# Block-sparse attention with a gated projection: the first weight chunks a unit later, fewer queries at first, and the loads of later batches spread over other units

## The chip, the cores and the metric

The kernel runs on one core of a Trainium2 chip. A time is device microseconds (us) of one launch. The core's engines are named as in the profile: PE (matrix multiplications, with PEld for its weight loads), DVE (the vector engine), ACT (the scalar engine), POOL (the general engine) and SP, which does no arithmetic and issues DMA transfers.

## The reference, cut to what matters

```python
# q, k, v: (B=4, H=8, S=768, D=64); 24 blocks of 32 rows
mask = np.abs(blk_i - blk_j) <= 1
mask = mask | (blk_i == 0) | (blk_j == 0) | (blk_i == n_blocks - 1) | (blk_j == n_blocks - 1)
for qb in range(n_blocks):
    for kb in sampled_blocks[qb]:                     # 3 of them
        mask[qb * block:(qb + 1) * block, kb * block:(kb + 1) * block] = True
scores = np.where(mask, scale * (q @ k^T), -1e9)
attn = softmax(scores)
x = (attn @ v).transpose(0, 2, 1, 3).reshape(B, S, 512)

gate_pre = sum(conv_w[k] * xp[:, k:k + S, :] for k in range(5))   # xp: x, padded by 4 rows ahead
gate = 1 / (1 + np.exp(-gate_pre))
out = (gate * (x @ w_val)) @ w_out                    # w_val, w_out: 512 x 512
```

A query block sees the two end blocks (0 and 23), its own neighbourhood and three sampled blocks. The two end blocks see everything. The result goes through a causal convolution over five rows that makes a gate, and two projections.

## The kernel before

**Units.** The work goes in 52 units. One unit is a pair of neighbouring query blocks with all eight heads; the two end blocks of a batch make two units of their own, which read all the keys and values of the batch. Batch 0 has units 0 to 12, with the end blocks first (0, 1). Batch 1 has 13 to 25, batch 2 has 26 to 38, batch 3 has 39 to 51; in these the end blocks come after four pairs (units 17 and 18, 30 and 31, 43 and 44). The step loop (L684 to L752) runs over units. In step n it issues loads, the scores of unit n, the copies of keys for unit n + 2 (COPY_AHEAD), the values of unit n - 2, and the transposes of unit n - 1; between these come the jobs of the gate and the projections (`fill`, `prepare`); then it scales the queries of unit n + 2.

**Order.** A small class (InOrder) chains every instruction to the one before it on its engine, so each engine runs its instructions in the order in which the program issues them. All instructions go through it, which is why they all have one line, L77, in the profile. A transfer issued by SP is given one of eight completion semaphores in turn, and its issue waits for the transfer that had that semaphore before, the eighth one back.

**Names.** `k` is the keys of a whole batch, in six chunks; `kg` the group of key blocks of one pair, copied from `k` by several engines. `vn` is the values of a whole batch, which the end blocks need, also in six chunks. `va` holds the value rows of a pair's own neighbourhood, in a ring of four; its first use of each buffer also loads the two end blocks' rows (a transfer of 64x1x520 ahead of one of 64x520). `vb` holds the gathered rows of the sampled blocks, fetched by POOL with an indirect DMA. `qc` is the queries of a pair (five buffers), `sc` and `s` scores, `mx` row maxima, `pe` exponentials, `pt` and `ptr` their transposes, `av` and `x` the attention output.

**Weights.** `w_val`, `w_out` and `conv_w` arrive as float64. Each of the eight 128-row chunks (`wst`, 128x1024 words, 512 KB) is turned on the DVE into a high and a low part (`wv`, `wo`) by the generator at L154, eight instructions on 128x512 per chunk, and one copy on ACT. Two chunks are worked on in turn, one step of each; the convolution's weights (`cst`) are first. A chunk's steps can begin DECODE_LAG units after its load was issued (L204 to L224), and the first step of all waits for a unit as well. `prepare(steps)` takes two steps at each of its two calls in a unit, three in units 2 to 6, so four or six in a unit. A chunk of `w_out` reuses the buffer of a chunk of `w_val` and is loaded when that one is decoded. When all are decoded, the same calls go on to the gate and the projection.

**Loads.** What is loaded when is set by tables of unit numbers: KEYS_AT (L32) for a batch's key chunks, ENDS_AT (L33) for its `vn` chunks, WEIGHTS_AT (L40) for the weight chunks. In unit 0 the first pair's keys are loaded and with them the queries of the first QUERIES_FIRST pairs (L41, used at L300); the loop `while more_keys()` at L703 then loads on as far as buffers go. From unit 1 on each step loads the keys, queries and values of the coming pairs as buffers come free.

Of the kernel before, what the change touches and what calls it, by code (L numbers as in the profile page):

```python
# [28 lines left out]
VRING, GRING = 4, 3  # L29

SIXTHS = 6
KEYS_AT = {1: (2, 2, 5, 5, 6, 6), 2: (15, 16, 17, 18, 19, 20), 3: (27, 28, 29, 30, 31, 32)}  # L32
ENDS_AT = {1: (9, 9, 10, 10, 13, 14), 2: (21, 22, 23, 24, 25, 26), 3: (34, 35, 36, 37, 38, 39)}  # L33

GLOB_AFTER = [-1] + [3] * (B - 1)
LAG_T, LAG_V = 1, 2
VALUES_AHEAD = 2

BUSY = (7, 1, 1)
WEIGHTS_AT = (0, 1, 3, 4, 7, 8, 11, 12)  # L40
QUERIES_FIRST = 5  # L41
DECODE_LAG = 3
SCALE_AHEAD = 2
COPY_AHEAD = 2

# [13 lines left out]
def attention_moe(ctx, tc, qb, kb, v, sampled, w_val, conv_w, w_out, ident_in, slot_in, out):  # L59
# [80 lines left out]
    def indices(b):  # L140

        row = const.tile([128, NB], F32, tag=f"row{b % 2}", name="row")
        dve.tensor_scalar_add(row, base, float(b * S - B * S))
        dve.tensor_tensor(out=row, in0=row, in1=valid, op=ALU.mult)
        dve.tensor_scalar_add(idx[:, b, :], row, float(B * S))
# [8 lines left out]
    def decode(hi, lo, raw, n):  # L154

        hw, lw = raw[:, :, 1], raw[:, :, 0]
        t = two.tile([128, DM], F32, tag="ot", name="words").bitcast(I32)[:, 0:n]
        dve.tensor_scalar(out=t, in0=hw, scalar1=0x1FF, scalar2=15, op0=ALU.bitwise_and, op1=ALU.logical_shift_left)
        yield True
        dve.scalar_tensor_tensor(  # L160
            out=lw.bitcast(U32), in0=lw.bitcast(U32), scalar=17, in1=t.bitcast(U32),
            op0=ALU.logical_shift_right, op1=ALU.bitwise_or,
        )
        yield True

        dve.tensor_scalar(out=t, in0=hw, scalar1=0x7FFFFFFF, scalar2=None, op0=ALU.bitwise_and)
        yield True
        dve.tensor_scalar(
            out=t.bitcast(F32), in0=t.bitcast(F32), scalar1=2.0**-15, scalar2=2.0**16, op0=ALU.max, op1=ALU.mult
        )  # L170
        yield True
        dve.tensor_scalar(out=t, in0=t, scalar1=3, scalar2=0x7FFFF000, op0=ALU.logical_shift_left, op1=ALU.bitwise_and)
        yield True
        dve.scalar_tensor_tensor(out=t, in0=hw, scalar=-(1 << 31), in1=t, op0=ALU.bitwise_and, op1=ALU.bitwise_or)
        yield True
        dve.tensor_scalar(out=hw, in0=t, scalar1=-(1 << 23), scalar2=None, op0=ALU.bitwise_and)
        yield True
        dve.scalar_tensor_tensor(out=lo, in0=lw, scalar=2.0**-35, in1=hw.bitcast(F32), op0=ALU.mult, op1=ALU.mult)
        act.copy(hi, t.bitcast(F32))
        yield True  # L180
# [15 lines left out]
    def decode_conv():  # L196
        yield from decode(cwp[:, 0, :], cwp[:, 1, :], cst, CH * KW)
        dve.tensor_tensor(
            out=cw.rearrange("p c k -> p (c k)"), in0=cwp[:, 0, :].bitcast(F32), in1=cwp[:, 1, :].bitcast(F32),
            op=ALU.add,  # L200
        )
        yield True

    def decode_weights():  # L204

        jobs, begun = [(-1, decode_conv())], 0
        while step[0] < DECODE_LAG - 1:
            yield False
        while jobs or begun < 2 * CH:
            n = begun  # L210
            if len(jobs) < 2 and n < 2 * CH and len(staged) > n and step[0] >= staged[n][0] + DECODE_LAG:
                dst = wv if n < CH else wo
                jobs.append((n, decode(dst[0][:, n % CH, :], dst[1][:, n % CH, :], staged[n][1], DM)))
                begun += 1
            if not jobs:
                yield False
                continue
            n, job = jobs.pop(0)
            if next(job, None):
                jobs.append((n, job))  # L220
                yield True
            else:
                decoded.add(n)
        decoded.add("all")  # L224
# [49 lines left out]
    def block_numbers(pr, eng):  # L274

        by = COPIED_FIRST if pr.seq < FIRST_PAIRS else COPIED[pr.bt.b]
        mine = [n for n in range(2 * NR) if by.get(n, SP) == eng]
        if not mine:
            return
        first = NR * PAIRS[pr.p][0] + mine[0]  # L280
        _, regs = nc.values_load_multi_w_load_instructions(
            sm[0:1, first : first + len(mine)], engines=[eng], min_val=0, max_val=NB - 1,
            skip_runtime_bounds_check_because="block numbers are drawn from [0, 24)",
        )
        for n, reg in zip(mine, regs):
            yield 5 + 4 * (n // NR) + n % NR, reg

    def load_queries(pr):
        pr.qc = five.tile([128, HP, 2, BLK], F32, tag="qc", name="qc")
        sp.dma_start(pr.qc, qb[:, pr.bt.b, pr.p + 1])  # L290

    def load_keys(pr):
# [3 lines left out]
        if pr is pairs[0]:  # L296
            for _ in range(3):
                next(keys_of[0])
            sp.dma_start(ident, ident_in)
            for other in pairs[1:QUERIES_FIRST]:  # L300
                load_queries(other)
# [314 lines left out]
    step, numbers_first = [0], {}  # L616
# [46 lines left out]
    def freed(k):  # L663

        return units[min(k, N - 1)].pr.seq if k >= 0 else -1

    def more(which, upto, load):
        if at[which] < len(pairs) and pairs[at[which]].seq <= upto:
            load(pairs[at[which]])
            at[which] += 1  # L670
            return True

    def until(which, n, do):
        while at[which] < min(len(pairs), pairs.index(units[min(n, N - 1)].pr) + 1):
            do(pairs[at[which]])
            at[which] += 1
# [7 lines left out]
    for n in range(N + LAG_V):  # L684
        step[0] = n

        def more_keys():
            return more("keys", freed(n - 1) + RING, load_keys)

        def more_values():  # L690
            free, soon = freed(n - LAG_V - 1), units[min(n + VALUES_AHEAD, N - 1)].pr.seq
            return (
                more("rows", min(free + VRING, soon), load_rows), more("gathered", min(free + GRING, soon), gather)
            )

        if n == 0:
            more_keys()
            indices(0)
            until("scaled", 1, scale)
            for _ in range(3):  # L700
                next(values_of[0])
            sp.dma_start(cst.rearrange("p n w -> p (n w)"), conv_w.bitcast(I32))
            while more_keys():  # L703
                pass
            more("rows", units[VALUES_AHEAD].pr.seq, load_rows)
            numbers_first.update({eng: list(block_numbers(pairs[1], eng)) for eng in (DVE, POOL, ACT)})
        else:
            while more_keys() or any(more_values()):
                more_values()
        store()  # L710
        for b in range(1, B):
            for at_units, loads in ((KEYS_AT[b], keys_of[b]), (ENDS_AT[b], values_of[b])):
                for _ in range(at_units.count(n)):
                    next(loads)
        k = len(staged)
        if k < 2 * CH and n >= WEIGHTS_AT[k] and (k < 4 or k - 4 in decoded):
            next(weights)

        if n == 0:
            none = ps_av.tile([128, 512], F32, tag="av", name="none")  # L720
            keep_busy(none, BUSY[0])
        if n < N:
            later = scores(units[n])
        until("copied", n + COPY_AHEAD, copy_keys)
        if n == 0:
            while any(more_values()):
                pass
        if 0 <= n - LAG_V < N:
            values(units[n - LAG_V])
        steps = STEPS + (n in MORE)  # L730
        if 0 <= n - LAG_T < N:
            for half, _ in enumerate(transposes(units[n - LAG_T])):
                if not (half and n in HELD):
                    fill()
                prepare(steps if half < 2 else 0)
            if later is not None:
                later()
        else:
            fill()
            prepare(steps)  # L740
        if 0 <= n - LAG_V < N and units[n - LAG_V].last:
            pr = units[n - LAG_V].pr
            finish(pr)
            pr.bt.done.add(pr.p)
            for t, (r0, rn) in enumerate(TILES[pr.bt.b]):
                need = {p for p in range(NP - 1) if any(r0 <= i * BLK < r0 + rn for i in PAIRS[p])}
                if r0 == 0 or r0 + rn == S:
                    need.add(-1)
                if t not in pr.bt.queued and need <= pr.bt.done:
                    pr.bt.queued.add(t)  # L750
                    queue_rows(pr.bt, t)
        until("scaled", n + SCALE_AHEAD, scale)  # L752
# [52 lines left out]
```

## Time and profile before

| | before |
|---|---|
| median of 3 runs | 402.39 us (400.53 to 403.91) |
| profiled execution: time | 400.56 us |
| profiled execution: span | 398.8 us |
| mean granted PE clock | 0.983 |
| PE busy | 350.2 us (88%) |
| PEld busy | 271.3 us (68%) |
| DVE busy | 283.9 us (71%) |
| ACT busy | 252.8 us (63%) |
| POOL busy | 238.0 us (60%) |
| moved by DMA | 67.15 MB, 168 GB/s in the mean |
| chain of work that ended last | PE 68%, DVE 17%, issue 7%, ACT 7% |

Busy time is that of instructions other than register, branch and DMA-issuing ones. The chain is followed back from the last instruction to whatever released each step; "issue" in it is time for which the profile names no releaser. The engines' shares are means over stages that differ: the weights are decoded in the first quarter alone.

### The profile page before, as it was taken

To read this page: it belongs to the slowest core of one execution; us is meant where nothing else is said; L and a number is where in the kernel's file an instruction comes from. 1 tells how busy PE (TensorE), PEld (TensorE's weight loads), DVE (VectorE), ACT (ScalarE), POOL (GpSimd) and SP (SyncE) were. 2 spreads that over 40 slices of the span, in tenths; PEclk is the share of its full clock that TensorE was granted. 3 is DMA by queue.
4 is the path that set the end of the run, shared out by engine and by line. 5 is a ranking of instruction groups with operands and counts; after the bars stand their busy time and mean duration, and the time that the engine had idled before them with its cause. 6 is when DMAs were issued, how large, how long until landed. Compare 5 with 4: busy or idle time off the path is not lost.

```text
span 398.8 us, 16127 instructions
## 1 busy us (share of the span) xinstructions
PE 350.2 (88%) x6616; PEld 271.3 (68%) x6616; DVE 283.9 (71%) x595; ACT 252.8 (63%) x610; POOL 238.0 (60%) x377
## 2 busy tenths in 40 slices
PE   8797867877687899899789989989989999899896
PEld 5474545654455787687568866976778788789694
DVE  4579997997879769677945784786584746957820
ACT  1487687876697868575555764775575665755521
POOL 2836776586479756826771677287646755522740
PEclk9889899998999999999999999999999999999999
DMA  7977899878745765885263557764733254120102
GB/s 246 341 211 237 263 288 284 263 232 258 214 122 164 214 161 157 247 263 150 55 180 103 148 156 207 215 190 122 196 108 103 62 147 111 53 79 26 54 26 80
DMA packets 41306, 67.15 MB, mean 168 GB/s; under 512 B 5649, under 2 KB 21905, under 8 KB 41233
## 3 DMA queue, kind: packets, MB, share of 16 engines
q1 hardware_dynamic: 34048, 42.67, 35.2%
q0 software_dynamic: 7040, 23.43, 20.8%
q8 instruction: 52, 0.85, 0.9%
q14 instruction: 22, 0.17, 0.1%
q10 hardware_dynamic: 144, 0.03, 0.0%
HBM read 59.81 MB, written 6.29 MB: 166 GB/s over the span
## 4 chain that ended last, share of the span: by engine, by line
PE 68%; DVE 17%; issue 7%; ACT 7%; POOL 1%; ACTq 0%; DVEq 0%; POOLq 0%
PE op L77 15%; PE vp L77 14%; PE av L77 13%; PE pt L77 11%; PE sc L77 9%; DVE mx L77 6%; DVE words L77 3%; PE s L77 3%; PE xp L77 2%; DVE th L77 2%; PE none L77 2%; ACT ptr L77 1%; DVE wst L77 1%; DVE x L77 1%; DVE rs L77 1%
## 5 line engine op out<-in xcount | busy, mean ns | idle before, releaser
L77 POOL DMA_INDIRECT vb<-in_v,idx x88 | 88.2, 1002 | 61.6 <-PE av L77 32.9
L77 DVE SCALAR_TENSOR_TENSOR th<-xT,cw,th 128x384 f32<-128x384 f32 x128 | 99.7, 793 | 14.3 <-ACT th L77 9.2
L77 ACT ACTIVATE pe<-sc,mx 128x256 f32<-128x256 f32 x176 | 69.0, 475 | 60.3 <-DVE mx L77 56.2
L77 DVE TENSOR_REDUCE mx<-sc 128x2 f32<-128x512 f32 x88 | 56.6, 684 | 47.9 <-PE sc L77 28.9
L77 POOL COPY kg<-k 128x128 f32 (+1 forms) x220 | 77.9, 395 | 7.6 <-DMA k<-in_k 7.4
L77 POOL TENSOR_TENSOR yl<-y,yh 128x384 fp32r<-128x384 f32 x32 | 35.3, 1103 | 63.5 <-ACT yh L77 63.5
L77 ACT COPY ptr<-pt 128x512 f32<-128x512 f32 x112 | 65.5, 600 | 12.1 <-PE pt L77 11.4
L77 PE MATMUL vp<-xh,wv 128*128 128x384 f32 x256 | 71.8, 345 | 0.0
L77 PE MATMUL av<-va,ptr 128*32 128x65 f32 x1408 | 51.6, 226 | 8.0 <-issue 7.4
L77 PEld LDWEIGHTS av<-va,ptr 128*32 128x32 f32 x1408 | 35.7, 111 | 28.9 <-issue 18.6
L77 PE MATMUL op<-wo,yh 128*128 128x512 f32 x192 | 54.7, 410 | 0.7 <-ACT yh L77 0.6
L77 PE MATMUL pt<-ident,pe 128*128 128x128 f32 x352 | 53.0, 283 | 1.4 <-ACT first L77 1.0
L77 PE MATMUL av<-vb,ptr 128*32 128x65 f32 x1408 | 48.9, 224 | 6.0 <-issue 5.8
L77 PE MATMUL sc<-kg,qc 64*32 64x256 f32 x1408 | 50.2, 391 | 0.0
L77 POOL TENSOR_TENSOR xl<-xT,xh 128x384 fp32r<-128x384 f32 x32 | 37.0, 1162 | 17.6 <-ACT xh L77 15.8
L77 PEld LDWEIGHTS vp<-xh,wv 128*128 128x128 f32 x256 | 46.8, 188 | 0.1
L77 PEld LDWEIGHTS pt<-ident,pe 128*128 128x128 f32 x352 | 39.8, 142 | 8.1 <-ACT first L77 1.2
L77 PE MATMUL vp<-xl,wv 128*128 128x384 f32 x128 | 43.0, 336 | 0.0
L77 PEld LDWEIGHTS av<-vb,ptr 128*32 128x32 f32 x1408 | 36.8, 111 | 8.2 <-issue 8.1
L77 PEld LDWEIGHTS op<-wo,yh 128*128 128x128 f32 x192 | 33.3, 189 | 6.8 <-ACT yh L77 1.7
L77 PE MATMUL xp<-ident,x 128*128 128x128 f32 x96 | 19.1, 281 | 14.6 <-DVE x L77 8.9
L77 PEld LDWEIGHTS sc<-kg,qc 64*32 64x32 f32 x1408 | 21.9, 107 | 13.9 <-issue 6.8
(75 smaller groups left out, 473.2 us busy)
## 6 DMA issues: line engine op xcount, KB each, us to landing
va<-in_v SPq DMA_DIRECT2D x60, 130.0 KB
qc<-in_q SPq DMA_DIRECT2D x48, 128.0 KB
out<-ot SPq DMA_DIRECT2D x24, 256.0 KB
kg<-in_k SPq DMA_DIRECT2D x77, 64.0 KB
vn<-in_v SPq DMA_DIRECT2D x18, 260.0 KB
k<-in_k SPq DMA_DIRECT2D x18, 256.0 KB
wst<-in_w_val SPq DMA_DIRECT2D x4, 512.0 KB
wst<-in_w_out SPq DMA_DIRECT2D x4, 512.0 KB
```

Of the source, the lines that this page charges most:

```text
L77: made = getattr(self.eng, name)(*args, **kwargs)
```

## The change

Four tables or numbers change, and two loops:

```diff
-KEYS_AT = {1: (2, 2, 5, 5, 6, 6), 2: (15, 16, 17, 18, 19, 20), 3: (27, 28, 29, 30, 31, 32)}
-ENDS_AT = {1: (9, 9, 10, 10, 13, 14), 2: (21, 22, 23, 24, 25, 26), 3: (34, 35, 36, 37, 38, 39)}
+KEYS_AT = {1: (5, 5, 6, 6, 9, 9), 2: (17, 18, 19, 20, 21, 22), 3: (27, 28, 29, 30, 31, 32)}
+ENDS_AT = {1: (13, 14, 15, 16, 17, 18), 2: (21, 22, 23, 24, 25, 26), 3: (34, 35, 36, 37, 38, 39)}
...
-WEIGHTS_AT = (0, 1, 3, 4, 7, 8, 11, 12)
-QUERIES_FIRST = 5
-DECODE_LAG = 3
+WEIGHTS_AT = (1, 2, 3, 4, 7, 8, 11, 12)
+QUERIES_FIRST = 3
+DECODE_LAG = 2
...
-        while step[0] < DECODE_LAG - 1:
+        while step[0] < DECODE_LAG:
...
-            while more_keys():
-                pass
+            for _ in range(2):
+                more_keys()
```

The first two weight chunks are loaded in units 1 and 2 instead of 0 and 1, and a chunk's decoding may begin two units after its load instead of three. The first decoding step stays in unit 2. The first unit asks for the queries of three pairs instead of five. The second batch's (1) key chunks and the third batch's (2) come later by the tables, as do the second batch's `vn` chunks. PE's order is unchanged; POOL's differs in one `xl` step of the later projection, ACT's in where its copies of the weights (`wv`, `wo`) and the gates' steps (`th`) stand. The rest is on SP and the DVE.

SP in units 0 to 3, before, with the semaphores that each issue waits for (the DMAHW ones belong to earlier transfers; the row of `qc` with PE and Activation waits for a buffer):

```order
L77 DMA cst<-in_conv_w 128x40 [waits DMAHW6_49]
L77 DMA wst<-in_w_val 128x1024 [waits DMAHW7_49]
L77 DMA va_119<-in_v 64x1x520 [waits DMAHW0_49]
L77 DMA va_119<-in_v 64x520 [waits DMAHW1_49]
L77 DMA va_120<-in_v 64x1x520 [waits DMAHW2_49]
L77 DMA va_120<-in_v 64x520 [waits DMAHW3_49]
L77 DMA wst<-in_w_val 128x1024 [waits DMAHW4_49]
L77 DMA va_121<-in_v 64x1x520 [waits DMAHW5_49]
L77 DMA va_121<-in_v 64x520 [waits DMAHW6_49]
L77 DMA k<-in_k 128x512 [waits DMAHW7_49]
L77 DMA k<-in_k 128x512 [waits DMAHW0_49]
L77 DMA qc<-in_q 128x256 [waits DMAHW1_49,PE_49,Activation_49]
```

And the same place after the change:

```order
L77 DMA cst<-in_conv_w 128x40 [waits DMAHW4_49]
L77 DMA va_119<-in_v 64x1x520 [waits DMAHW5_49]
L77 DMA va_119<-in_v 64x520 [waits DMAHW6_49]
L77 DMA qc<-in_q 128x256 [waits DMAHW7_49]
L77 DMA va_120<-in_v 64x1x520 [waits DMAHW0_49]
L77 DMA va_120<-in_v 64x520 [waits DMAHW1_49]
L77 DMA qc<-in_q 128x256 [waits DMAHW2_49]
L77 DMA wst<-in_w_val 128x1024 [waits DMAHW3_49]
L77 DMA va_121<-in_v 64x1x520 [waits DMAHW4_49]
L77 DMA va_121<-in_v 64x520 [waits DMAHW5_49]
L77 DMA wst<-in_w_val 128x1024 [waits DMAHW6_49]
L77 DMA qc<-in_q 128x256 [waits DMAHW7_49,PE_49,Activation_49]
```

The first chunk moved from ahead of `va_119` to behind `va_120`, the second from behind `va_120` to behind `va_121`, two queries in between, and the two chunks of `k` are gone from here.

SP in units 9 and 10, before (`sm` is the table of sampled block numbers, read into registers):

```order
L77 DMA va_119<-in_v 64x520
L77 DMA vn<-in_v 128x520 x2
L77 DMA qc<-in_q 128x256
L281 TENSOR_LOAD sm
L77 ISA
L77 DMA kg_118<-in_k 128x128
L77 DMA va_120<-in_v 64x520
L77 DMA vn<-in_v 128x520 x2
L77 DMA qc<-in_q 128x256
```

And after:

```order
L77 DMA va_119<-in_v 64x520
L77 DMA k<-in_k 128x512 x2
L77 DMA qc<-in_q 128x256
L281 TENSOR_LOAD sm
L77 ISA
L77 DMA kg_118<-in_k 128x128
L77 DMA va_120<-in_v 64x520
L77 DMA qc<-in_q 128x256
```

Unit 9 has the last two key chunks of batch 1 where two of `vn` were, and unit 10 has none.

The DVE in unit 17, the last weight chunk, before (the four rows from `words` on are the decoding, the `mx` rows the next row maxima, buffer numbers kept):

```order
L77 RECIPROCAL rs_2254<-rs_2254 128x4
L77 TENSOR_TENSOR x_2257<-av_2221,rs_2254 128x256
L77 TENSOR_SCALAR words_2032<-words_2032 128x512
L77 SCALAR_TENSOR_TENSOR words_2032<-wst_1584,words_2032 128x512
L77 TENSOR_SCALAR wst_1584<-words_2032 128x512
L77 SCALAR_TENSOR_TENSOR wo1_126<-wst_1584 128x512
L77 TENSOR_REDUCE mx_2316<-s_2290 128x1
```

And after:

```order
L77 RECIPROCAL rs_2252<-rs_2252 128x4
L77 TENSOR_TENSOR x_2255<-av_2219,rs_2252 128x256
L77 SCALAR_TENSOR_TENSOR words_1937<-wst_1580,words_1937 128x512
L77 TENSOR_SCALAR wst_1580<-words_1937 128x512
L77 SCALAR_TENSOR_TENSOR wo1_126<-wst_1580 128x512
L77 TENSOR_REDUCE mx_2319<-s_2293 128x1
```

One decoding step fewer is left for this unit; unit 9 takes four steps instead of three.

## The prediction

> **What bounds the kernel now.** I read the busy time by stages first, then the chain of waits, then the queues that the change touches. The windows give for each stretch its length, the busy us (and instructions) of PE, PEld, DVE, ACT and POOL, the granted clock, the DMA share and GB/s:
>
> ```profile
> 0.00:20.00 20.00, 15.72 (x148) 9.87 (x156) 10.37 (x42) 6.67 (x14) 10.35 (x23) 0.91 0.90 293
> ...
> 30.00:60.00 30.00, 22.24 (x618) 15.04 (x602) 28.39 (x57) 23.14 (x69) 21.54 (x35) 0.94 0.89 264
> 60.00:70.00 10.00, 7.63 (x211) 5.15 (x209) 7.28 (x16) 7.23 (x22) 6.87 (x13) 1.00 0.92 283
> ...
> 120.00:360.00 240.00, 222.96 (x4145) 178.11 (x4144) 169.68 (x339) 154.58 (x363) 149.04 (x231) 1.00 0.52 149
> ```
>
> From 120 to 360 PE is busy 223 of 240 us; there the change alters neither PE's order nor a load, up to two chunks of keys near 120. Whatever it does, it does ahead of that, and the later stages carry it along. From 30 to 60 the DVE is busy 28.4 of 30 us, and the chain of waits (start, length, what) runs through its decoding of the weights, without a break:
>
> ```profile
> 33.44 1.46 DVE words L77 x3
> 34.91 0.80 DVE wst L77
> 35.71 1.69 DVE words L77 x2
> ...
> 42.69 0.43 DVE wst L77
> ```
>
> So between 30 and 60 us a load matters only if it makes the DVE wait. From 60 to 70 the DVE has 2.7 us of idle time, and the first 20 us have both a full DMA side (0.90) and little work done.
>
> **The start.** PE's and POOL's timelines (start, length, what, and idle time before it with what ended it):
>
> ```profile
> 14.82 0.49 PE L77 MATMUL pt<-ident,first 128*128 128x128 f32 x3 [0.43 <-issue]
> 17.20 1.22 PE L77 MATMUL pt<-wo 128*128 128x256 f32 x2 [1.89 <-ACT ptr L77]
> ...
> 19.20 1.96 PE L77 MATMUL sc<-kg,qc 64*32 64x256 f32 x32
> 21.27 2.42 PE L77 MATMUL av<-vn,ptr 128*32 128x65 f32 x96
> ...
> 25.60 1.09 PE L77 MATMUL sc<-kg,qc 64*32 64x256 f32 x32
> 26.62 1.57 PE L77 MATMUL av<-vn,ptr 128*32 128x65 f32 x96
> ...
> 14.48 0.95 POOL L77 DMA_INDIRECT vb<-in_v,idx  x1 [0.30 <-issue]
> ```
>
> PE loses 2.3 us between 14.4 and 17.2 (0.43 and 1.89 idle). The rows name no transfer. While it crawls, POOL issues a gather, and the change moves none of them: POOL's order is the same until far behind the start. Nothing that the first units read (the first keys, the first queries) stands behind a moved transfer. I cost the start at 0. The bounds are 0 and -4.0: the 2.3 us, and the score and value matmuls behind them at the rate that the same ones have some 6 us later, 0.87 us (1.96 against 1.09) and 0.85 us (2.42 against 1.57) less.
>
> **First weight chunks a unit later, two queries later, two key chunks out of unit 2.** No transfer is added. SP's timeline, and what SP waited for from 28.9 to 31:
>
> ```profile
> 10.25 0.46 SPq L77 DMA_DIRECT2D wst<-in_w_val  x1
> ...
> 13.70 1.63 SPq L77 DMA_DIRECT2D wst<-in_w_val  x1
> 16.08 6.89 SPq L77 DMA_DIRECT2D va<-in_v  x2
> ...
> 28.95 1.10 SPq L77 DMA_DIRECT2D va<-in_v  x2
> 30.83 0.33 SPq L77 DMA_DIRECT2D wst<-in_w_val  x1
> 34.05 0.33 SPq L77 DMA_DIRECT2D qc<-in_q  x1
> 34.44 1.25 SPq L77 DMA_DIRECT2D wst<-in_w_val  x1
> ...
> SPq L77 <- DMA wst<-in_w_val: 0.8, 1, 0.8
> ```
>
> Each issue waits for the landing of the eighth transfer before it (the listing above shows the eight semaphores). So these rows date landings. The third chunk at 30.83 waited for the second one (issued at 13.70): that took 17 us to land. The pair at 28.95 waited for the second pair of values; the issues at 34.05 and 34.44 stood behind the two transfers of the third pair. Landings come in the order of issue. The change keeps the transfers ahead of these points the same as a set and permutes them: the first chunk now stands last behind the second pair of values, the second chunk last behind the third pair. So the first chunk should land when that second pair landed, near 29.5 (28.95 to 30.05), and the second chunk when the third pair did, by 34.44. The DVE wants them here:
>
> ```profile
> 29.08 0.42 DVE L77 TENSOR_SCALAR words<-wst 128x512 int32<-128x512 int32 x1
> ...
> 30.97 0.18 DVE L77 TENSOR_TENSOR cw<-cwp 128x20 f32<-128x20 f32 x1 [0.73 <-ACT cwp L77]
> ...
> 33.69 0.48 DVE L77 TENSOR_SCALAR words<-wst 128x512 int32<-128x512 int32 x1
> ```
>
> The first chunk comes 0.4 us late, and the 0.73 us that the DVE waits for ACT at 30.97 hides that. The second comes up to 0.75 us late (34.44 against 33.69), with nothing to hide it: behind it on the DVE stand the rest of the decoding and the row maxima of the next unit, for which ACT's exponentials wait. I take +0.5, between 0 (34.05 was set by another wait) and 0.75. The third chunk is wanted a unit earlier, at the last of six steps of unit 5; it is issued near 30.8 as before with two key chunks fewer ahead of it, and I cost it at nothing because the DVE reaches that step only at 42.69 (the chain's row above), 12 us on. The fourth has a like margin. The two queries are scaled at 26 us and later, behind transfers that landed by then: 0.
>
> The Trainium skill, DMA: Bandwidth & Descriptors, section "Why a DMA increments its semaphore by 16 and not by 1", says that a transfer runs on as many of the 16 engines as divide its slowest dimension, up to 16. By that rule the two end rows of the values (two times 32 rows) run on two engines, and all that is issued behind them finishes there last; it speaks against putting the chunks behind them, the 17 us agree, and the sum would take the upper end, +0.75.
>
> **Second batch's loads later.** Two of its key chunks move from unit 2 to unit 9, four chunks of its values from units 9 and 10 to units 15 to 18, and the third batch's keys two units on. Unit 9 trades two chunks for two of the same size: 0. Unit 10 loses two (260 KB each). PE and DVE there (the chain of waits first, then the DVE's timeline), and SP's issue of the two chunks:
>
> ```profile
> 63.80 1.52 issue
> ...
> 63.54 1.29 DVE L77 TENSOR_REDUCE mx<-sc 128x2 f32<-128x512 f32 x2 [0.59 <-PE sc L77]
> ...
> 66.15 0.16 DVE L77 TENSOR_SCALAR rs<-av 128x4 f32<-128x4 f32 x1 [1.32 <-PE av L77]
> ...
> 60.56 1.12 SPq L77 DMA_DIRECT2D vn<-in_v  x2
> ```
>
> PE stands 1.52 us at 63.80 in the middle of a unit's value matmuls, that is, for gathered rows that have not landed, just behind the two chunks of 60.56. The DVE loses 0.59 + 1.32 = 1.9 us. Without the chunks the gather shares the DMA engines with less. Bounds 0 and -1.9; I take -0.8, about half of the stall, since other transfers remain.
>
> The last value chunk now goes out where SP issues at about 102.8, one more transfer behind the 102.13 row, and PE reads it from 111.98:
>
> ```profile
> 86.91 1.14 SPq L77 DMA_DIRECT2D va<-in_v  x2
> ...
> 99.71 0.48 SPq L77 DMA_DIRECT2D va<-in_v  x1
> ...
> 102.13 0.58 SPq L77 DMA_DIRECT2D k<-in_k  x1
> ...
> 111.98 0.66 PE L77 MATMUL av<-vn,ptr 128*32 128x65 f32 x32
> ```
>
> That is 9.2 us ahead: 0. The upper end is 3.6: the transfers of 86.91 landed by 99.71, eight issues on, so within 12.8 us. The third batch's keys are complete by unit 22 and first copied at unit 24: two units of cover, 0.
>
> **Decoding one step ahead.** In unit 9 the DVE does four steps instead of three, and so one less in unit 17. The extra step (0.42, like the row at 29.08) lies in the 0.59 us of idle time at 63.54. In unit 17 the DVE works without a gap from the first of four steps to the next row maximum:
>
> ```profile
> 102.80 0.63 DVE L77 TENSOR_SCALAR words<-words 128x512 int32<-128x512 int32 x1
> 103.46 0.76 DVE L77 SCALAR_TENSOR_TENSOR words<-wst,words 128x512 int32<-128x512 int32 x1
> ...
> 105.94 1.02 DVE L77 TENSOR_REDUCE mx<-s 128x1 f32<-128x512 f32 x2
> ```
>
> The 0.63 us goes; PE's end blocks may set that place instead. Bounds 0 and -0.63; I take -0.5, nearer to the row. The gates begin one step earlier with it; that finds no wait of its own.
>
> **Sum.** +0.5 - 0.8 - 0.5 = -0.8. The profiled execution took 400.56 (span 398.8), so 399.8 there; the median of the three runs is 1.83 above it, so 401.6. The ends of the terms, +0.75 and -2.5, make 399.9 to 403.1; with 0.8 us to either side for the runs' own spread (400.53 to 403.91), 399.1 to 403.9.
>
> **The rivals.**
> - The start was held by the DMA side after all, and the lighter queue frees it: -4.0 in place of 0, and no late second chunk (-0.5): 397.1. For it speaks the DMA share of 0.90; against it that PE's slow rows stand beside gathers and name no transfer, and that the decode would have to get its chunks some 4 us earlier than the queue allows. The Trainium skill, TensorE: Matmul & The Clock Gate, part 1, says that PE runs at half its clock after an idle window of about 3.4 us; the granted clock of 0.91 in the first window agrees, and by the rule a start without the stall gains the slow stretch too. Chance 0.14.
> - The second chunk takes as long to land as the one that it follows did: 17.1 us from issue (13.70 to 30.83), counted from the end of the issue ahead of it, 22.97. Then it lands at 40.1, 6.4 us after 33.69, and the DVE stands still with the row maxima behind it: 401.6 - 0.5 + 6.4 = 407.5. Against it: the 17 us were mostly the queue ahead of it, which is shorter by then. It decides from a landing at about 38.5 on (4.8 us late). Chance 0.08.
> - The last value chunk is 3.6 us late at unit 19: 405.2. Chance 0.06.
> - The change does not reach a bound: the late chunk is hidden, the gather waits as long as before and unit 17 follows PE: 402.4. Chance 0.2.
>
> **Numbers.** The forecast has 0.52, and it and the last rival lie within 1%, 4.0 us, about what a measurement of this kernel can tell from no change. Faster than 398.4: 0.14 from the start and 0.03 from the lower edge of the forecast, 0.17. Slower than 406.4: 0.08, and 0.03 from a larger mishap with the values, 0.11. The same: 0.72. A range with 8 in 10 takes in the freed start, 397.1, with some margin (396.6), and the late values, 405.2, and leaves out the 17 us chunk and small tails.
>
> **What would show it.** In the new profile: the second chunk's first DVE step with idle time before it that a DMA ended, 0 to 0.8 us (several us is the second rival); PE at 14 us with the same crawl (gone is the first rival); the stall near 64 us half as long or less; no wait of PE before the end blocks' value matmuls near 112. The forecast is wrong if the start runs through, or if the decode's stage from 30 to 60 us comes out longer than before by more than 1 us.

## The result and the profile after

| | before | after |
|---|---|---|
| median of 20 runs | 402.42 us (400.53 to 407.38) | 399.83 us (397.13 to 403.76) |
| ratio | | 0.9923, 95% interval 0.9900 to 0.9947 |
| profiled execution: time, span | 400.56, 398.8 us | 400.60, 398.8 us |
| DVE idle ahead of the gate's steps (`th`) | 14.3 us | 6.4 us |

The changed kernel is faster by 0.77%, some 3 us, with an interval of 0.53 to 1.0%. The medians are of all runs; this kernel has a second, slower state, and the ratios here leave the runs in it out, so they are not quite the quotients of the medians. The forecast was a change of -0.8 us within a range that holds the measured time. The two profiled executions have the same span: that of before lies below the median of its kernel, that of after above its own. So no single pair of profiles carries the difference, and the places have to be compared one by one.

The page and the windows of the changed kernel (length, busy us and instructions of PE, PEld, DVE, ACT, POOL, granted clock, DMA share, GB/s):

```profile
PE 349.5 (88%) x6616; PEld 271.4 (68%) x6616; DVE 284.3 (71%) x595; ACT 251.7 (63%) x610; POOL 237.9 (60%) x377
```

```profile
0.00:20.00 20.00, 14.74 (x148) 8.96 (x156) 9.55 (x41) 6.47 (x13) 10.14 (x23) 0.95 0.90 288
...
30.00:60.00 30.00, 21.29 (x625) 14.87 (x602) 28.59 (x61) 23.51 (x69) 24.27 (x37) 1.00 0.94 280
60.00:70.00 10.00, 7.48 (x212) 5.17 (x212) 9.83 (x20) 8.00 (x25) 7.91 (x15) 1.00 0.76 228
...
120.00:360.00 240.00, 223.47 (x4113) 178.84 (x4105) 167.94 (x333) 151.95 (x359) 143.66 (x224) 0.99 0.51 149
```

The DVE's 2.7 us of idle time from 60 to 70 are gone (9.83 of 10 us busy, 7.28 before; 8.72 in a second profile of the changed kernel), at 228 GB/s instead of 283. The start and the stage from 30 to 60 take as long as they did.

To compare places I number the outputs: the instruction with which the DVE begins to close a pair's attention (`rs` from `av`), from 0 to 47; output 16 is that of the second batch's end blocks. Start of some outputs, us:

```
output            2       5       7      12      15      16      24      25      33      34      47
before        38.51   55.08   66.15   89.58  108.76  120.17  170.84  176.69  250.03  256.70  357.98
after         38.44   54.46   63.98   87.29  107.64  117.76  168.26  175.49  249.83  257.70  358.06
```

The changed kernel is 2.2 us ahead at output 7 and 2.4 us at output 16. It lost that again between outputs 24 and 25 (1.4 us), between 33 and 34 (1.2 us). The second profile of the changed kernel, taken later, has 5.64 us instead of 7.23 between 24 and 25, so that loss is one execution's. The loss between 33 and 34 is not: that profile has 7.87 us there, too.

The stretch from output 15 to 16 is 11.41 us before and 10.12 after. The DVE's timeline there, before and then after (start, length, what, idle time before it):

```profile
109.16 0.43 DVE L77 TENSOR_TENSOR x<-av,rs 128x256 f32<-128x256 f32 x1
110.65 2.55 DVE L77 SCALAR_TENSOR_TENSOR th<-xT,cw,th 128x384 f32<-128x384 f32 x3 [1.06 <-ACT th L77]
113.12 1.28 DVE L77 TENSOR_REDUCE mx<-sc 128x2 f32<-128x512 f32 x2
...
119.11 1.14 DVE L77 COPY kg<-k 128x128 f32 x1
```

```profile
108.04 0.42 DVE L77 TENSOR_TENSOR x<-av,rs 128x256 f32<-128x256 f32 x1
108.38 3.20 DVE L77 SCALAR_TENSOR_TENSOR th<-xT,cw,th 128x384 f32<-128x384 f32 x4
111.50 1.28 DVE L77 TENSOR_REDUCE mx<-sc 128x2 f32<-128x512 f32 x2
...
117.49 0.30 DVE L77 COPY kg<-k 128x128 f32 x1
```

The `th` rows are the gate's first steps. Before, ACT makes their starting values (`th`) just ahead of them, and the DVE waits 1.06 us for the first, which ends at 110.61. After, the gate begins one call earlier and the wait is gone; one more step fits in, and the row maxima (`mx`) start 0.50 us sooner behind output 15 (3.86 us instead of 4.36). The other 0.79 us lie in the key copy (`kg`), the last thing on the DVE ahead of output 16: 1.14 us before, 0.30 after. Before, two `xl` steps run on POOL from 118.19 to 120.14, the second alongside the copy; after, there is one, from 116.70 to 117.70, and the copy begins just ahead of its end. That `xl` step is the one in which POOL's order differs. That it holds the copy up fits the times, but was not tried by itself. The same row of the costliest groups, on the page of before and of after (busy us, mean ns, idle time before it and its main releaser):

```profile
L77 DVE SCALAR_TENSOR_TENSOR th<-xT,cw,th 128x384 f32<-128x384 f32 x128 | 99.7, 793 | 14.3 <-ACT th L77 9.2
```

```profile
L77 DVE SCALAR_TENSOR_TENSOR th<-xT,cw,th 128x384 f32<-128x384 f32 x128 | 97.8, 767 | 6.4 <-ACT th L77 3.6
```

This row is the mark of the order of steps. The idle time in it is 13.6 to 14.3 us in all five profiles that have the DVE's old order, on either kind of chip (more on the chips below), and 6.4 us in all eight that have the new one. It is a wait that comes back, not one at a single place. The DVE's idle time ahead of the first gate step behind an output, where it is over 0.15 us (at 19 and 24 the first profile of before names no releaser, at the others ACT's `th`):

```
behind output      15     19     24     28     33     38     43     47
before           1.06   1.35   1.77   1.01   2.08   1.43   1.24   2.37
after               -      -      -      -      -      -   1.25   2.37
```

### A wait that the profile does not name

PE stops at 57.7 and at 63.8 us (of the second the forecast spoke) with no releaser but "issue". PE's timeline of before, and the page's row of the DMA queue that moves instructions (packets, MB, share):

```profile
59.03 0.24 PE L77 MATMUL av<-va,ptr 128*32 128x65 f32 x1 [1.31 <-issue]
...
65.32 0.26 PE L77 MATMUL av<-vb,ptr 128*32 128x65 f32 x3 [1.52 <-issue]
```

```profile
q8 instruction: 52, 0.85, 0.9%
```

Both stops lie in the middle of a run of matmuls. Counting PE's recorded instructions (a matmul and its weight load are two), the first after the stop is number 1985 and number 2241, counted from 0: 256 apart. The queue's 52 packets are 16 KB each; 52 times 256 is 13,312, and the trace has 13,414 instructions of PE. In before the packets run from 56.45 to 57.57 and from 62.57 to 63.81, and PE goes on 1.46 and 1.50 us after their end. So I read the stops as PE waiting for the next 256 instructions of its program. On this reading number 256k - 63 begins a piece (from k = 3 on and over the first 170 us; instructions that the trace doesn't record shift it later). If its packet is asked for when PE begins the piece ahead (an assumption; over these pieces no packet begins before that), the two packets stood 4.8 and 3.5 us in the queue in before, and 3.3 and 2.5 us in after, where the same two stops are 0.15 and 0.2 us. The Trainium skill, Runtime: NRT & Kernel Launch, section "Instruction fetch mechanics", has the same 16 KB blocks of 256 instructions and calls the cost of crossing one mostly hidden; the trace agrees with the size, and here the crossing costs up to 5.1 us.

PE's time from one start to the next at three such borders, in all profiles:

```
kernel               chip     at 1985   at 2241   at 2753
before               401 us     1.5       1.7       0.1
before, again        401        1.1       1.2       0.1
after                401        0.15      0.2       0.1
after, again         401        1.3       0.0       0.1
decode_alone         401        1.9       0.0       4.6
values_back_2        401        1.4       1.2       0.1
old_decode_again     401        1.9       0.0       0.1
gates_two            401        1.1       0.4       0.1
heavy                401        1.0       1.9       2.5
after_spread         401        0.0       0.0       0.15
start_alone          385        1.5       1.6       5.1
tables_alone         385        1.7       1.3       5.1
old_decode_order     385        1.6       0.0       3.9
values_back          385        1.5       2.7       4.3
```

(The chips differ: the kernel before takes 385.5 us on the chip of the first four experiments, and 400.7 to 402.4 us where the result and the other experiments were measured, here called the 401 us chips. A ratio is always against the kernel before on the same chip.)

### The profile page after: what moved, and what is told of

Same layout as the page of the kernel before. It is cut to its first block, busy times and chain, and to the rows that moved or that the text cites. A ratio compares the mean times of both kernels' runs of the same rounds, so it can differ in the third digit from the quotient of the medians.

```text
span 398.8 us, 16126 instructions
## 1 busy us (share of the span) xinstructions
PE 349.5 (88%) x6616; PEld 271.4 (68%) x6616; DVE 284.3 (71%) x595; ACT 251.7 (63%) x610; POOL 237.9 (60%) x377
## 3 DMA queue, kind: packets, MB, share of 16 engines
HBM read 59.81 MB, written 6.29 MB: 166 GB/s over the span
## 4 chain that ended last, share of the span: by engine, by line
PE 57%; DVE 19%; DMA 8%; ACT 7%; issue 6%; another core or an unknown queue 1%; POOL 1%; SPq 1%; ACTq 0%; DVEq 0%
PE op L77 15%; PE vp L77 14%; PE av L77 10%; PE pt L77 8%; PE sc L77 7%; DVE mx L77 7%; DVE words L77 4%; DMA va<-in_v 3%; DMA wst<-in_w_val 3%; DVE wst L77 2%; DVE th L77 2%; PE xp L77 2%; DMA k<-in_k 2%; PE s L77 1%; ACT ptr L77 1%
## 5 line engine op out<-in xcount | busy, mean ns | idle before, releaser
L77 POOL DMA_INDIRECT vb<-in_v,idx x88 | 89.2, 1013 | 56.6 <-PE av L77 29.6
L77 DVE SCALAR_TENSOR_TENSOR th<-xT,cw,th 128x384 f32<-128x384 f32 x128 | 97.8, 767 | 6.4 <-ACT th L77 3.6
L77 PE MATMUL vp<-xh,wv 128*128 128x384 f32 x256 | 72.6, 348 | 0.7 <-DVE y L77 0.7
L77 PE MATMUL pt<-ident,pe 128*128 128x128 f32 x352 | 53.9, 286 | 1.0 <-issue 1.0
L77 PE MATMUL sc<-kg,qc 64*32 64x256 f32 x1408 | 49.3, 388 | 0.0
L77 POOL TENSOR_TENSOR xl<-xT,xh 128x384 fp32r<-128x384 f32 x32 | 35.2, 1105 | 18.8 <-ACT xh L77 17.0
```

Of the source, the lines that this page charges most:

```text
L77: made = getattr(self.eng, name)(*args, **kwargs)
```

## The experiments

**The change in two halves.** Theories at first: A, the loads taken out of units 9 and 10 carry the gain; B, the lighter queue at the start carries it. First half alone:

```diff
-WEIGHTS_AT = (0, 1, 3, 4, 7, 8, 11, 12)
-QUERIES_FIRST = 5
-DECODE_LAG = 3
+WEIGHTS_AT = (1, 2, 3, 4, 7, 8, 11, 12)
+QUERIES_FIRST = 3
+DECODE_LAG = 2
...
-        while step[0] < DECODE_LAG - 1:
+        while step[0] < DECODE_LAG:
...
-            while more_keys():
-                pass
+            for _ in range(2):
+                more_keys()
```

> The change's first half alone: weight chunks a unit later, decoding two units after a load, three queries at first, two key loads of unit 0; the tables of keys and values are those of before. Theory A (the gain of 2.6 us comes from the loads taken out of units 9 and 10): no gain, ratio to before 0.998 to 1.002, and PE's two gaps near 58 and 64 us (1.31 and 1.52 us in the profile of before) remain, at the same places of PE's program. Theory B (the gain comes from the start, whose shorter queue lets all later transfers go out earlier): most of the gain, ratio 0.992 to 0.995, and the two gaps are gone or under 0.5 us together.

Measured: 382.42 against 385.49 us, ratio 0.9914 (0.9882 to 0.9945). Second half alone:

```diff
-KEYS_AT = {1: (2, 2, 5, 5, 6, 6), 2: (15, 16, 17, 18, 19, 20), 3: (27, 28, 29, 30, 31, 32)}
-ENDS_AT = {1: (9, 9, 10, 10, 13, 14), 2: (21, 22, 23, 24, 25, 26), 3: (34, 35, 36, 37, 38, 39)}
+KEYS_AT = {1: (5, 5, 6, 6, 9, 9), 2: (17, 18, 19, 20, 21, 22), 3: (27, 28, 29, 30, 31, 32)}
+ENDS_AT = {1: (13, 14, 15, 16, 17, 18), 2: (21, 22, 23, 24, 25, 26), 3: (34, 35, 36, 37, 38, 39)}
```

> The other half alone: the second batch's keys and values and the third batch's keys over the later units, the start as before. Theory A (loads out of units 9 and 10): ratio 0.992 to 0.995 and both gaps near 58 and 64 us gone. Theory B (the start): ratio 0.998 to 1.002, the gap near 58 us stays and the one near 64 us is at most halved.

Measured: 383.21 us, 0.9936 (0.9908 to 0.9965). Both halves alone are faster, and both keep both stops (1.5 and 1.6 us, 1.7 and 1.3 us). Neither theory foresaw a gain with the stops still there. What tells the profiles of that chip apart is another place: from output 15 to 16 start_alone takes 10.12 us and tables_alone 11.41. The first half contains the DVE's new order of steps. That is theory C: the order carries the gain, through the gates that begin a call earlier. It does not explain tables_alone, which has the old order and all eight waits and is faster than before all the same.

**The old order in the changed kernel.**

```diff
-            if len(jobs) < 2 and n < 2 * CH and len(staged) > n and step[0] >= staged[n][0] + DECODE_LAG:
+            if len(jobs) < 2 and n < 2 * CH and len(staged) > n and step[0] >= staged[n][0] + DECODE_LAG + (n > 1):
```

The DVE's instructions stand as in the kernel before, all loads as after.

> The changed kernel with the DVE's order of before: from the third weight chunk on the decoding may begin three units after the load instead of two, so unit 9 has three steps and unit 17 four again, and the gates begin one step later. If the step saved in unit 17 is worth what the prediction gave it, the time is 0.5 to 0.6 us above that of the changed kernel (ratio to before 0.9935 to 0.995); if it is covered, the ratio is that of the changed kernel, 0.992. In the profile the time from the last pair's output of unit 14 to that of the end blocks shows it directly.

Measured: 384.45 us, 0.9977 (0.9944 to 1.0010), and from output 15 to 16 it takes 11.45 us. On this chip the order shows clearly in the profiles: from output 14 to the end of the span the two of the old order (tables_alone, old_decode_order) take 283.4 us each, the two of the new one (start_alone, values_back) 279.6 and 279.4 us. So tables_alone gained nothing there that this run lacks; what it gained, if it did, lies ahead of that, and the two intervals overlap (0.9944 to 0.9965). Run once more on a chip of the other kind:

> The changed kernel with the DVE's order of before, once more, beside the others of this call. Theory C (the order carries the gain): ratio 0.997 to 1.001, the stretch between the outputs 15 and 16 is 11.4 us. Theory A or B (the loads carry it): ratio 0.992 to 0.996.

Measured: 399.74 against 400.71 us, 0.9973 (0.9937 to 1.0009). Here output 15 to 16 took 13.59 us, since PE also crept through the end blocks' values for 2.2 us beside two gathers on POOL. Without the new order about 1 us of gain is left in both runs, and both intervals reach past 1. So some of the gain may be the loads'; the runs can't tell.

**The new order in the kernel before.**

```diff
-            if len(jobs) < 2 and n < 2 * CH and len(staged) > n and step[0] >= staged[n][0] + DECODE_LAG:
+            if len(jobs) < 2 and n < 2 * CH and len(staged) > n and step[0] >= staged[n][0] + DECODE_LAG - (n > 1):
```

DVE, ACT and POOL then have the changed kernel's order, and no transfer moves. The kernel before and the changed kernel ran beside it:

> The kernel before once more, for its profile beside the others of this call: PE's program comes in pieces of 256 instructions, and PE's gaps at the pieces' borders should be there again (two near 58 and 64 us on the first chip). If this is another chip than that of the first profiles, the stretch from 120 us on may be shorter, as it was in the four runs before (360 to 383 us in all).

> The changed kernel once more, as the anchor of the others: ratio to before 0.990 to 0.995. If the change is two independent parts (the step order of the decoding, and a shorter queue), its ratio lies near that of the first half alone (0.991) and below that of the tables alone (0.994).

> The kernel before with one edit: from the third weight chunk on the decoding may begin two units after the load, so DVE, ACT and POOL have the changed kernel's order and every transfer that of before. Theory C (the order of the steps carries the gain, through the gates that begin a call earlier): the stretch from the first to the second output after the end blocks of batch 1 is 10.1 us instead of 11.4, and the ratio is 0.991 to 0.995. Theory A or B (the queue carries it): the stretch may shrink, but the ratio stays at 0.997 to 1.001.

Measured: the kernel before 401.59 us, its profile with stops of 0.89 and 0.96 us idle at the same two numbers; the changed kernel 398.96, 0.9935 (0.9902 to 0.9968); the order alone 399.49, 0.9935 (0.9905 to 0.9966). The stretch from output 15 to 16 (the end blocks' own output, not the one behind them as the expectation's words have it) is 10.12 us in both, and 11.40 in before. One edit of the order gives the whole gain of the changed kernel, within the intervals. Its profiled execution (401.80 us) is above that median; two stops of PE, at numbers 1985 and 2753, take 6 us in it:

```profile
60.04 0.32 PE L77 MATMUL av<-va,ptr 128*32 128x65 f32 x1 [1.64 <-issue]
...
79.98 1.09 PE L77 MATMUL pt<-ident,pe 128*128 128x128 f32 x6 [4.34 <-issue]
```

**The value chunks back in units 9 and 10.**

```diff
-ENDS_AT = {1: (13, 14, 15, 16, 17, 18), 2: (21, 22, 23, 24, 25, 26), 3: (34, 35, 36, 37, 38, 39)}
+ENDS_AT = {1: (9, 9, 10, 10, 13, 14), 2: (21, 22, 23, 24, 25, 26), 3: (34, 35, 36, 37, 38, 39)}
```

> The changed kernel with the second batch's value chunks back in units 9 and 10 (two each) and 13, 14; unit 9 then has two key and two value chunks. Theory A (loads out of units 9 and 10): the gap near 64 us comes back, 1.3 us or more, ratio to before 0.996 to 1.0. Theory B (the start): the ratio stays within 0.991 to 0.995 and PE has no gap over 0.5 us between 55 and 68 us.

> The changed kernel with the value chunks back in units 9 and 10, once more, since it was the fastest of its call (0.9878). If the value chunks' place does nothing, the ratio is that of the changed kernel, 0.992 to 0.994, and PE's gap at instruction 2241 is there without a cost in the end; if leaving them was a gain that the first call showed by chance, 0.995 or more.

Measured: 380.55 us, 0.9878 (0.9840 to 0.9915) on the 385 us chip, the lowest ratio of all; 398.77 us, 0.9948 (0.9914 to 0.9982) on the other. The stop at number 2241 is back, 2.7 and 1.2 us, as theory A has it, but the time does not follow: the two intervals barely touch, one ratio below and one above the changed kernel's 0.9923 to 0.9935 (which was not run on the 385 us chip). Whether moving these chunks gains or loses is not settled.

**The end rows over more engines.** Theory D: PE's packets wait behind the end blocks' rows, which go over two DMA engines alone (such a transfer has one or two landing events in the trace, the others 16 or nearly).

```diff
-            sp.dma_start(vt[0:64, :], ends)
+            for e in range(2):
+                sp.dma_start(vt[32 * e : 32 * e + 32, :], ends[e])
```

> The changed kernel with each transfer of the two end blocks' rows (64x1x520) sent as two of 32x520. Theory D (PE waits at the borders of its program's pieces for the next piece, a transfer of 16 KB that stands behind these rows, which two of the sixteen engines carry alone): the gaps at PE's borders under 80 us (2 to 5 us each on the chip of the last call) fall to under 1 us each, the rows land within 5 us of their issue instead of 10 or more, and the time is 2 to 6 us less than the changed kernel's. If the gaps come from the load on all engines, they stay, and the time is within 1 us of it.

Measured: 399.74 us, 0.9960 (0.9925 to 0.9995), no gain on the changed kernel's 0.9935. The end rows do land sooner by the trace's landing events (issued at 16.86, landed at 26.56, 9.7 us; in the changed kernel 16.21 and 31.12, 14.9 us), and the fourth weight chunk lands at 33.8 instead of 43.0. But the same bytes then crowd 20 to 30 us. The windows of the changed kernel (second profile) and of this one:

```profile
20.00:30.00 10.00, 8.80 (x302) 6.47 (x294) 7.39 (x23) 8.57 (x23) 3.63 (x14) 0.98 0.64 195
30.00:60.00 30.00, 22.07 (x608) 15.90 (x593) 28.03 (x57) 23.11 (x68) 22.83 (x35) 0.91 0.92 274
```

```profile
20.00:30.00 10.00, 6.13 (x240) 4.44 (x226) 5.55 (x15) 8.58 (x23) 3.34 (x13) 1.00 0.97 277
30.00:60.00 30.00, 23.62 (x654) 16.76 (x646) 26.74 (x61) 21.52 (x63) 20.64 (x34) 0.94 0.73 236
```

PE's stops moved with the crowd, all at numbers 256k - 63 (or one on): 705, 961, 1217 and 3009.

```profile
29.60 0.99 PE L77 MATMUL av<-vn,ptr 128*32 128x65 f32 x51 [2.36 <-issue]
34.98 0.26 PE L77 MATMUL av<-va,ptr 128*32 128x65 f32 x4 [1.38 <-issue]
...
40.90 0.25 PE L77 MATMUL av<-va,ptr 128*32 128x65 f32 x2 [1.21 <-issue]
...
83.58 1.07 PE L77 MATMUL sc<-kg,qc 64*32 64x256 f32 x24 [1.97 <-issue]
```

So spreading the rows did not free the packets, and theory D fell in that form. That the packets wait behind all that is queued fits the places and is not shown further.

**Six transfers more.** If the packets wait behind all that is queued, a longer queue makes PE stop for longer.

```diff
+    twice = load_all_values(batches[1], SIXTHS)
...
+        for _ in range((8, 8, 9, 9, 10, 10).count(n)):
+            next(twice)
```

> The changed kernel with six transfers more: the second batch's value chunks (260 KB each) are also loaded in units 8, 9 and 10, two in each, into their own buffer, and once more in units 13 to 18 as before; what is computed stays the same. Theory D2 (PE stands still at the borders of its program's 256-instruction pieces when the next piece, 16 KB, is late behind the backlog of all loads): the wait of the next pieces in the queue grows from 1 to 4 us to 5 us or more at borders 8 to 10 (PE's instructions 1985, 2241, 2497), PE's gaps there sum to 4 to 9 us instead of 0.4 to 1.4, and the time rises by 2 to 6 us (ratio to before 0.998 to 1.008). Rival (PE waits for gathered rows or for the DVE): no gap over 0.5 us at these borders, and what PE loses stands ahead of value matmuls of vb or of the transposes.

Measured: 400.24 against 400.71 us, 1.0003 (0.9967 to 1.0040). The changed kernel was not run on this chip; by its ratios on two others (0.9923, 0.9935) this is about 3 us above it, and the intervals just touch. PE's stops at 1985, 2241 and 2497 sum to 3.0 us and not the 4 to 9 expected, the packets waiting 4.2, 4.0 and 1.7 us; the largest came one border later, at 2753 (2.5 us), and one of 2.2 us at 4289, in the end blocks' values.

```profile
64.42 0.26 PE L77 MATMUL av<-vb,ptr 128*32 128x65 f32 x3 [1.63 <-issue]
...
76.37 1.54 PE L77 MATMUL pt<-ident,pe 128*128 128x128 f32 x6 [2.23 <-issue]
```

All stops over 0.3 us at the borders of the first 20 pieces are 7.5 us in this profile and 1.3 in the changed kernel's second one. So with six transfers that nothing waits for, PE's stops at the borders of its program grew. How much of the 3 us goes that way is not shown.

**The gates earlier still.**

```diff
-STEPS, MORE = 2, (*range(2, 7), *range(48, 53))
+STEPS, MORE = 2, (*range(2, 7), 10, *range(48, 53))
```

> The changed kernel with three decoding steps instead of two at each call of unit 10, so that the decoding ends and the gates begin two steps earlier still. Theory C (the earlier gates carry the gain): the stretch between the outputs 15 and 16 stays at 10.1 us or falls, later stretches fall too, and the time is 0.5 to 2 us below the changed kernel's (ratio 0.988 to 0.992). Rival (the DVE has no room left in unit 10): that unit is 1.3 us longer, units 11 and 12 shorter by as much, and the time stays within 0.5 us.

Measured: 402.73 us, 1.0026 (0.9987 to 1.0066): by the ratios slower than the changed kernel by some 3 us, against both expectations. The DVE's timeline ahead of the end blocks, here and then in the changed kernel (second profile):

```profile
102.81 0.68 DVE L77 SCALAR_TENSOR_TENSOR wo<-wst 128x512 fp32r<-128x512 int32 x1
104.47 1.89 DVE L77 SCALAR_TENSOR_TENSOR th<-xT,cw,th 128x384 f32<-128x384 f32 x2 [0.98 <-ACT th L77]
106.29 0.68 DVE L77 TENSOR_REDUCE mx<-s 128x1 f32<-128x512 f32 x1
108.16 0.42 DVE L77 TENSOR_REDUCE mx<-s 128x1 f32<-128x256 f32 x1 [1.19 <-PE s L77]
```

```profile
103.72 1.16 DVE L77 SCALAR_TENSOR_TENSOR wo<-wst 128x512 fp32r<-128x512 int32 x1
104.80 0.68 DVE L77 TENSOR_REDUCE mx<-s 128x1 f32<-128x512 f32 x1
105.81 0.42 DVE L77 TENSOR_REDUCE mx<-s 128x1 f32<-128x256 f32 x1 [0.33 <-PE s L77]
```

Two gate steps, and a wait of 0.98 us for ACT, now stand ahead of the end blocks' row maxima; PE waits 2.15 us for ACT's `xT` copy (1.24 in the first profile of the changed kernel), and the maxima wait for PE. From output 14 to 15 it takes 10.46 us instead of 6.57, and 13.24 instead of 10.12 to output 16, where PE also crept beside two gathers; over 95 to 120 us its granted clock is 0.82 (1.00 in the changed kernel's second profile), and a row of score matmuls at 115.16 takes 1.96 us instead of 1.09. The waits are back at eight places, the first six one output earlier, and the row of the costliest groups has more of them than before:

```profile
L77 DVE SCALAR_TENSOR_TENSOR th<-xT,cw,th 128x384 f32<-128x384 f32 x128 | 97.4, 769 | 16.3 <-ACT th L77 12.6
```

So earlier is not better as such; the gain of the change is the place of one step, and one step further it is lost.

## Why the prediction was right, and where it was not

- **The start, 0.** Right. PE crawls as before. In the changed kernel's PE timeline:

```profile
15.31 0.33 PE L77 MATMUL pt<-ident,first 128*128 128x128 f32 x1 [0.86 <-issue]
...
17.70 0.92 PE L77 MATMUL pt<-wo 128*128 128x256 f32 x2 [0.53 <-issue]
...
19.41 1.96 PE L77 MATMUL sc<-kg,qc 64*32 64x256 f32 x32
```

  The scores that began at 19.20 begin at 19.41. The value matmuls behind them took 1.57 us instead of 2.42, one of the pieces that the rival had priced, but PE then waited 0.82 us for ACT, and output 0 is 0.1 us sooner. The rival of the freed start did not happen.

- **The second weight chunk, +0.5 (0 to 0.75).** Right in mechanism, too large. The DVE's timeline:

```profile
30.84 0.18 DVE L77 TENSOR_TENSOR cw<-cwp 128x20 f32<-128x20 f32 x1 [0.73 <-ACT cwp L77]
...
33.85 0.43 DVE L77 TENSOR_SCALAR words<-wst 128x512 int32<-128x512 int32 x1 [0.21 <-DMA wst<-in_w_val]
```

  It waits 0.21 us for the chunk, which landed at 33.83 by the trace's events, near the 34.44 that the queue's order gave. Output 2 comes at 38.44 against 38.51, so nothing of it is left. The 17 us rival did not happen. The rule that the prediction named from the Trainium skill, DMA: Bandwidth & Descriptors, agrees with the run that sent the end rows as two transfers (14.9 to 9.7 us to land); the +0.75 us that the sum would take by it did not come.

- **The stall at 63.80, -0.8 (0 to -1.9).** The place was right, the cause was not. I took it for gathered rows that had not landed; PE had passed its waits for both gathers of the unit, at 63.27 and 63.47, and by the packets' times it waited for its own program. The step that failed is the reading of "issue" in the middle of value matmuls. The stop went in the profile (1.52 to 0.2 us), and the one at 57.72, of which the forecast had no term, went too; in the second profile of the changed kernel that one is there again (1.3 us), the one at 63.80 not. The chunks out of unit 10 fit: the stop at 2241 is 1.2 us or more in six of the seven profiles with value chunks there, and 0 to 0.4 us in six of the seven without (heavy, with its extra chunks, counts among the first). What it is worth in time stays open, between 0 and some 1.5 us, since values_back gave both signs.

- **The last value chunk, 0.** Right: the end blocks' value matmuls begin at 110.85 with no wait ahead of them.

- **Decoding one step ahead, -0.5 in unit 17, and "the gates begin one step earlier with it; that finds no wait of its own".** This is the step that failed, and the one that carries the result. The step itself took 0.13 us off (6.70 to 6.57 us from output 14 to 15). The gates' earlier start took 1.29 us off from output 15 to 16 (11.41 to 10.12), 0.50 us of it at the wait for ACT ahead of 110.65, a row that the trace of before showed and that I did not follow. Mis-sized: -0.5 where the profiles have -1.4 by output 16. The runs give the order alone -2.6 us (1.4 to 3.8).

- **"Whatever it does, it does ahead of that" (of the stretch from 120 to 360 us).** Wrong with it. The same wait comes back behind outputs 19, 24, 28, 33 and 38, that is, between 120 and 360 us, and goes at all five. What that is worth differs by place and chip. On the 385 us chip the stretches from 33 to 34 and 38 to 39 lost 1.12 and 0.37 us, and all between outputs 16 and 47 2.4 us (222.0 against 224.4 us in two profiles each). On the 401 us chips the stretch from 38 to 39 lost as much (6.66 to 6.29 us in both second profiles), but the one from 33 to 34 grew from 6.66 to between 7.8 and 7.9 us in all six profiles of the new order: the wait of 2.08 us is gone, and the DVE stands 2.38 us just ahead of the output instead (second profile of the changed kernel; no releaser in the trace). Between 16 and 47 nothing is left there (238.30 us in before, 238.23 in after, 238.40 with the order alone, in profiles of one chip). So on those chips the profiles place some 1.5 us of the 2.6, by output 16; the rest is not located.

- **The sum.** -0.8 was forecast, -2.6 to -3.1 measured. "The same" by the bound of 1% was the likely case and came true because the gain stayed below it, not because the terms were right: the range held by its width.

## What to carry to other kernels

Where a list of jobs runs on one engine in program order, moving one job moves all behind it: follow the first job of the next list too, and look in the trace of before at what it waits for, there and at every later place where the list comes round again. A stop of PE with no releaser in the middle of equal matmuls can be its program arriving late: count instructions from one stop to the next, and if they are 256 apart, look at what is queued on the DMA engines ahead of that (from the assumed request to PE going on it was 5 to 10 us here). Comparing profiles by the start of each output shows which stretches are the kernel's own (from output 15 to 16, 10.11 to 10.13 us in seven of the eight profiles of the new order; the eighth, heavy, has a stop at a border there) and which are one execution's.

## What the runs showed of the hardware

PE's program, as I read the instruction queue, comes in packets of 16 KB on the same DMA engines as the data. At each stop of 0.9 us or more at a border, in all profiles, PE goes on 1.2 to 1.6 us after such a packet's end, and it lost up to 5.1 us from one start to the next. That can be a cost of loads which nothing waits for.

The chips differ: 385.5 us on one, 400.7 to 402.4 on the others, for the same kernel. On these PE creeps in steps of about 0.7 us while POOL issues gathers: from 120 to 360 us each of their ten profiles has 18 to 22 places where two value matmuls start 0.5 to 0.9 us apart, 11.7 to 14.1 us together, nearly all during a gather. The four profiles of the 385 us chip have none, with as much time in gathers (52 to 53 us). The page's rows of PE's value matmuls, of before on the first chip and of start_alone on the 385 us chip:

```profile
L77 PE MATMUL av<-va,ptr 128*32 128x65 f32 x1408 | 51.6, 226 | 8.0 <-issue 7.4
...
L77 PE MATMUL av<-vb,ptr 128*32 128x65 f32 x1408 | 48.9, 224 | 6.0 <-issue 5.8
```

```profile
L77 PE MATMUL av<-va,ptr 128*32 128x65 f32 x1408 | 48.0, 229 | 3.0 <-issue 2.8
...
L77 PE MATMUL av<-vb,ptr 128*32 128x65 f32 x1408 | 46.5, 226 | 1.4 <-issue 1.4
```

What makes PE creep there was not tried.
